# Retention followed by soft mixture-of-experts attention: scaling and transposing the probabilities one step later, with gates, decay, values and the tail rearranged

## The chip, the cores and the metric

One core of one Trainium2 chip. The time is the device time of one execution in microseconds (us), the median of three runs. The core has engines that run their own instruction queues in order: PE (TensorE, matrix products; PEld is its weight load), DVE (VectorE), ACT (ScalarE), POOL (GpSimd) and SP (SyncE, which issues the DMA transfers here). Matrix products land in PSUM, which has eight banks in this kernel; a bank can be used again once its reader has finished.

## The reference

```python
def _attn_ref(q, k, v):                      # 8 batches, 8 heads, 576 tokens, head_dim 64
    scores = scale * np.matmul(q, k.transpose(0, 1, 3, 2))
    gamma = 1.0 - 2.0 ** (-5.0 - np.arange(H))
    Dmat = np.where(rel >= 0, gamma[:, None, None] ** rel, 0.0)
    return np.matmul(scores * Dmat, v)

def _moe_ref(x, w_gate, wq, wk, wv, wo):     # x: (8, 576, 512), 4 experts of width 64
    logits = x @ w_gate                      # the two best experts of each token, softmax over them: w
    for e in range(E):
        q, k, v = x @ wq[e], x @ wk[e], x @ wv[e]
        scores = np.where(causal, -1e9, scale * (q @ k.transpose(0, 2, 1)))
        a = softmax(scores)
        ye = a @ v @ wo[e]
        out += mask[..., None] * w * ye      # where expert e is one of the two
```

All data is 32-bit float. The first half (retention) gives x; the second half (four experts' causal attention with gates) gives the output.

## The kernel before, in words

Each batch of 576 tokens is cut into five chunks (four of 128 tokens, one of 64). The main loop has a step n for each of the 40 chunks, and every instruction of PE, DVE, ACT and POOL runs in the order in which the program writes it; only DMA issues on SP are placed by the compiler.

A step does, in this order. `qk(n)` forms the chunk's retention scores (line 137), ACT copies them out of PSUM as `p` (line 140), POOL masks them (line 143). `result(n-1)` finishes the chunk before: products `old` with the running state and `own` with the chunk's values (lines 165, 178), ACT copies `old` (line 168), DVE adds `own` (line 183), POOL multiplies by the decay table (line 188), ACT rounds to `xh` (line 189) and POOL forms the rest `xl` (line 191). `state(n)` adds the chunk to the running state (PE line 117, DVE lines 123 and 125); it needs `decay(n)`, a POOL multiplication of the chunk's v (line 104) that was written a step earlier, behind line 191. Six steps behind (`LAG = 6`) `scores(n-6)` forms the expert scores `ss` of an attention tile m (line 334, the 64-row tile line 341); DVE masks them and takes maxima (lines 352, 356), ACT takes exponentials with sums (line 360). Then `gates()` runs the whole gate chain on DVE with one ACT exponential in its middle (lines 289 to 308). Then `spread(m)`: three small DVE operations form the factors `rs` (lines 372 to 374), the four expert parts of `p32` are scaled, half on ACT (line 378) and half on DVE (line 380), and DVE transposes them in 32-blocks into the constant tiles TA and TB (lines 385, 387). The scaling is written ahead of the step's remaining PE work, the transposes between its parts.

That PE work (`work(n)`) repeats with five steps for each batch. Five letters name the steps in the text: step K1 (n mod 5 = 1) has the projections kq1 of tokens 256 to 575 (line 233), and the attention values of the batch before (`values`, line 398, evacuated by ACT line 406 and DVE line 407); step V1 (n mod 5 = 2) has the value projections v1 (line 258, evacuated by ACT line 262 and, for the gate logits `lg`, by DVE line 263) and the output projection o0 (line 418, evacuated by ACT line 421); step K0 (n mod 5 = 3) has kq0; step O (n mod 5 = 4) has the output projection o1; step V0 (n mod 5 = 0) has v0. The attention tile of steps K1, V1, K0, O, V0 has t = 0, 1, 2, 3, 4, and its score rows have 64 to 576 elements. In a step with `values` the transposes wait until the values are done, since both use TA. After step 41 a hand-written `end()` takes the last batch's tiles in the order 3, 4, 2.

Of the kernel before, what the change touches and what calls it, by code (L numbers as in the profile page):

```python
# [33 lines left out]
def kernel(ctx: ExitStack, tc: tile.TileContext, xf, xt, vkf, vkt,  # L34
# [111 lines left out]
    def result(n):  # L146
# [39 lines left out]
        yield  # L186
        e = gp if n > 1 else v
        e.tensor_mul(x32, x32, gi[:, :, t0:t0 + C])  # L188
        act(xh[:, :, l0:l0 + C], x32, AF.Copy)  # L189
        yield  # L190
        e.tensor_sub(xl[:, :, l0:l0 + C], x32, f(xh[:, :, l0:l0 + C]))  # L191
# [51 lines left out]
    def vproj(b, r, t):  # L243
# [18 lines left out]
        act(vn[:, ti], ps[:, :E * D], AF.Copy)  # L262
        v.tensor_copy(lg[:, ti], ps[:, E * D:])
        if t == tiles[-1]:
            GATES.append((b, r))

            hv = hbm.tile([128 * nt, E * D], F32, name=f"hv{r}")
            nc.sync.dma_start(hv.rearrange("(t p) c -> p t c", p=128), vn)
            for g in range(4):
                p = g // 2  # L270
                nc.sync.dma_start(vq[QUAD[g]], hv[:, 128 * p:128 * p + 128].rearrange("(j r) c -> r j c", r=32))
# [3 lines left out]
    GATES = []  # L275

    def gates():
        while GATES:
            gate(*GATES.pop())

    def gate(b, r):
        nt = len(RNG[r][2])
# [14 lines left out]
        ex = sb.tile(sh2, F32, name="ex", tag="ex")  # L297
        v.tensor_sub(ex, lg, mx[:, 0].unsqueeze(2).to_broadcast(sh2))
        act(ex, ex, AF.Exp)
        v.scalar_tensor_tensor(ex, rk, 1.5, ex, op0=OP.is_lt, op1=OP.mult)  # L300
        v.tensor_reduce(mx[:, 1], ex, axis=AX.X, op=OP.add)
        v.tensor_scalar(mx[:, 1], mx[:, 1], 1e-9, None, op0=OP.add)
# [62 lines left out]
    def spread(m):  # L365
        b, t = divmod(m, 5)
        r = 0 if t < 2 else 1
        ti = t - RNG[r][2][0]
        p32, sm, ws = SS.pop(m)
        n = len(ws)  # L370
        rs = sm[:, 1, :n]
        v.tensor_scalar(sm[:, 0, :n], sm[:, 0, :n], 1e-9, None, op0=OP.add)
        v.reciprocal(rs, sm[:, 0, :n])
        v.tensor_mul(rs, rs, WT[b, r][:, ti].rearrange("p i z -> p (i z)")[:, :n])  # L374
        for u in range(n):
            x = p32[:, u, :ws[u]]
            if u % 2:
                act(x, x, AF.Copy, scale=rs[:, u:u + 1])  # L378
            else:
                v.tensor_scalar(x, x, rs[:, u:u + 1], None, op0=OP.mult)  # L380
        yield
        for u in range(n):
            z, k, nb = u % 2, 2 * t + u // 2, ws[u] // 32
            x = p32[:, u, :ws[u]].rearrange("p (j c) -> p j c", c=32)
            v.transpose(TA[:, :min(nb, 8), z, k], x[:, :min(nb, 8)])  # L385
            if nb > 8:
                v.transpose(TB[:, :nb - 8, z, k - 4], x[:, 8:])
            yield
# [37 lines left out]

    STEPS = {}
    for b in range(B):
        late = b == B - 1

        for n, kind in ((5 * b + 3, "kq0"), (5 * b + 5 - late, "v0"), (5 * b + 6, "kq1"), (5 * b + 7, "v1"),
                        (5 * b + 11, "y"), (5 * b + 12, "o0"), (5 * b + 14, "o1")):
            if b or kind[-1] == "1" or kind in ("o0", "y"):
                STEPS.setdefault(n, []).append((b, kind, None))
    for n in STEPS:
        STEPS[n].sort(key=lambda x: "kvyo".index(x[1][0]))

# [3 lines left out]
    def work(n):  # L441
        vals = [values(b, 0, 9) for b, kind, part in STEPS.get(n, []) if kind == "y"]
        for b, kind, part in STEPS.get(n, []):
# [3 lines left out]
            if kind[:-1] == "kq":  # L447
                for p in range(2) if part is None else [part]:
                    for w in "kq":
                        yield from proj(b, r, w, p)  # L450
                        for y in vals:
                            next(y, None)
            elif kind[:-1] == "v":
                for t in RNG[r][2] if part is None else [part]:
                    yield from vproj(b, r, t)
            else:
                for d in range(4):
                    yield from outproj(b, r, d)

    def run(g):  # L460
        for _ in g:
            pass


    LAST = NC - 5
    TILES = {n: [n - LAG] for n in range(LAG, NC + 1)}
    TILES[NC].append(LAST)
    TILES[NC + 1] = [LAST + 1]

    def end():  # L470
        b = B - 1
        run(scores(LAST + 3))
        for t in RNG[1][2]:
            run(vproj(b, 1, t))
        for d in range(4):
            run(outproj(b - 1, 0, d))
        gates()
        run(spread(LAST + 3))
        run(scores(LAST + 4))
        for d in range(4):  # L480
            run(outproj(b - 1, 1, d))
        run(spread(LAST + 4))
        run(scores(LAST + 2))
        run(values(b, 0, 4))
        for d in range(4):
            run(outproj(b, 0, d))
        run(spread(LAST + 2))
        run(values(b, 4, 9))
        for d in range(4):
            run(outproj(b, 1, d))  # L490

    warm(12)
    load(0)
# [5 lines left out]
    for n in range(NC + 2):  # L499
# [3 lines left out]
            nc.sync.dma_start(mask[:, 448:], con_d[:, 92:])  # L503
        if n in (1, 4):
            fetch("v" if n == 1 else "o")
        new = TILES.get(n, [])
        late = result(n - 1) if 1 <= n <= NC else iter(())
        if n < 3:

# [7 lines left out]
        else:  # L517
# [2 lines left out]
            next(late, None)  # L520
            if n < NC:
                state(n)
        for m in new[:1]:
            run(scores(m))
        if n > 5:
            run(late)
        decay(n + 1)
        gates()
        for w in {2: "kq", 3: "v", 6: "o"}.get(n, ""):
            weights(w, "l" if w == "k" else "hl")  # L530
        for m in new[1:]:
            run(scores(m))
        new = {NC: new[:1], NC + 1: [LAST] + new}.get(n, new)
        spreads = (None for m in new for _ in spread(m))
        next(spreads, None)
        hold = any(kind == "y" for _, kind, _ in STEPS.get(n, []))
        for _ in work(n):
            if not hold:
                next(spreads, None)
        run(spreads)  # L540
        run(late)
    end()


def _layout(inputs):
# [51 lines left out]
```

## Time and profile before

| | us |
|---|---|
| median of 3 runs | 508.36 |
| lowest and highest | 505.86, 508.96 |
| the profiled execution | 509.4 |
| its span in the trace | 507.7 |

The span runs from the first to the last instruction; 1.7 us of the profiled execution lie around it. In the rows below, PEclk is the granted clock of TensorE as a share of 2.4 GHz; it takes only the two levels 1.0 (2.4 GHz) and 0.5 (1.2 GHz), and a number between them is a mean over a stretch. Square brackets in a timeline give an engine's idle time ahead of the instruction and what ended it.

### The profile page before, as it was taken

How to read it: one execution, taken by the hardware profiler on the slowest of the kernel's cores; microseconds unless marked ns; L12 is line 12 of the kernel's file. 1: busy time of each engine (PE TensorE's matmuls, PEld its weight loads, DVE VectorE, ACT ScalarE, POOL GpSimd, SP SyncE). 2: the span in 40 equal slices, each digit the busy share in tenths (PEclk: the TensorE clock that was granted, in tenths of full speed). 3: DMA queues.
4: the chain of work that ended last, by engine and by line, in shares of the span. 5: the costliest groups of instructions: out<-in, count | busy, mean ns of one | idle time of the engine just before them, and what ended most of it. 6: DMA issues, size and time to landing. Idle time of an engine off the chain costs nothing. (4 is left out here: it accounts for less than half of the span.)

```text
span 507.7 us, 21336 instructions
## 1 busy us (share of the span) xinstructions
PE 434.3 (86%) x9068; PEld 375.5 (74%) x9068; DVE 343.8 (68%) x1275; ACT 258.7 (51%) x802; POOL 174.8 (34%) x198
## 2 busy tenths in 40 slices
PE   6498885799897998699898998699997998889866
PEld 3497873689676997589767897589866886778655
DVE  3744798746888377857788477866788478846750
ACT  2455546526464476536565366536475355645442
POOL 2437354414345233433354143433344153200000
PEclk9579997799998999989988999989988998979879
DMA  8937275214744155433735065432845031300621
GB/s 290 357 104 255 86 178 168 74 35 159 203 151 117 50 160 181 155 89 113 225 113 180 13 200 178 136 107 85 221 138 175 15 105 34 116 3 3 159 70 54
DMA packets 49246, 66.73 MB, mean 131 GB/s; under 512 B 4096, under 2 KB 38400, under 8 KB 49152
## 3 DMA queue, kind: packets, MB, share of 16 engines
q1 hardware_dynamic: 49152, 65.38, 41.1%
q8 instruction: 71, 1.16, 1.0%
q14 instruction: 23, 0.19, 0.1%
HBM read 50.68 MB, written 14.68 MB: 129 GB/s over the span
## 5 line engine op out<-in xcount | busy, mean ns | idle before, releaser
L360 ACT ACTIVATE p<-p,nm 128x64 f32<-128x64 f32 (+6 forms) x144 | 79.5, 553 | 96.6 <-DVE nm L352 65.1
L143 POOL TENSOR_SCALAR_AFFINE_SELECT p<-p 64x512 f32<-64x512 f32 (+1 forms) x80 | 50.1, 626 | 152.2 <-ACT p L140 149.5
L378 ACT ACTIVATE p<-p,sm 128x320 f32<-128x320 f32 (+8 forms) x72 | 36.9, 555 | 62.7 <-DVE sm L374 62.7
L380 DVE TENSOR_SCALAR p<-p,sm 128x320 f32<-128x320 f32 (+8 forms) x72 | 54.2, 789 | 1.4
L352 DVE CUSTOM_DVE_ANT_0 p<-ss,mask 128x128 f32<-128x128 f32 (+7 forms) x128 | 51.0, 452 | 2.8 <-PE ss L334 2.6
L385 DVE STREAM_TRANSPOSE ta<-p 128x256 f32<-128x256 f32 (+2 forms) x144 | 49.8, 368 | 4.4 <-ACT p L378 4.1
L188 POOL TENSOR_TENSOR x<-x,gi 128x512 f32<-128x512 f32 (+1 forms) x38 | 44.3, 1166 | 22.4 <-DVE x L183 17.6
L183 DVE TENSOR_TENSOR x<-x,own 128x256 f32<-128x256 f32 (+1 forms) x80 | 26.1, 358 | 38.1 <-ACT x L168 37.9
L178 PE MATMUL own<-p,vk 64*64 64x64 f32 x1152 | 32.5, 232 | 21.5 <-ACT k L238 14.0
L334 PE MATMUL ss<-k,q 64*64 64x512 f32 (+7 forms) x512 | 48.2, 470 | 2.3 <-DVE nm L356 1.6
L191 POOL TENSOR_TENSOR x1l<-x,x1h 128x512 fp32r<-128x512 f32 (+1 forms) x24 | 26.4, 1099 | 65.6 <-ACT x1h L189 65.6
L407 DVE TENSOR_TENSOR yl<-ys,yh 128x288 fp32r<-128x288 f32 (+2 forms) x36 | 12.8, 416 | 52.1 <-ACT yh L406 52.1
L117 PE MATMUL st<-vk 64*64 64x64 f32 x1024 | 26.1, 232 | 24.4 <-POOL vk L104 14.7
L178 PEld LDWEIGHTS own<-p,vk 64*64 64x64 f32 x1152 | 27.4, 143 | 24.2 <-issue 19.0
L117 PEld LDWEIGHTS st<-vk 64*64 64x64 f32 x1024 | 22.1, 143 | 26.3 <-POOL vk L104 15.4
L398 PE MATMUL ys<-ta,vq 32*64 32x256 f32 (+8 forms) x1152 | 34.7, 369 | 3.8 <-DVE ta L385 2.0
L398 PEld LDWEIGHTS ys<-ta,vq 32*64 32x64 f32 x1152 | 25.6, 141 | 12.2 <-issue 6.9
L104 POOL TENSOR_TENSOR vk<-vk,con 128x512 f32<-128x512 f32 (+1 forms) x34 | 33.4, 984 | 0.1
L418 PE MATMUL po<-yh,who 128*128 128x320 f32 (+1 forms) x128 | 29.6, 312 | 3.3 <-ACT yh L406 3.3
L421 ACT ACTIVATE ot<-po 128x256 f32<-128x256 f32 (+1 forms) x64 | 24.0, 407 | 15.4 <-PE po L418 12.3
L334 PEld LDWEIGHTS ss<-k,q 64*64 64x64 f32 x512 | 23.1, 151 | 9.3 <-DVE nm L356 2.9
L140 ACT ACTIVATE p<-qk 128x256 f32<-128x256 f32 (+1 forms) x80 | 24.7, 368 | 9.9 <-PE qk L137 9.9
(106 smaller groups left out, 1040.1 us busy)
## 6 DMA issues: line engine op xcount, KB each, us to landing
x<-xf SPq DMA_DIRECT2D x32, 512.0 KB, 4.3
vk<-vkf SPq DMA_DIRECT2D x32, 512.0 KB, 5.4
vq<-hv SPq DMA_DIRECT2D x32, 192.0 KB, 4.7
out<-ot SPq DMA_DIRECT2D x32, 160.0 KB, 1.9
vq<-hv SPq DMA_DIRECT2D x32, 128.0 KB, 3.5
out<-ot SPq DMA_DIRECT2D x32, 128.0 KB, 2.5
hv<-vn SPq DMA_DIRECT2D x8, 384.0 KB, 2.9
ta<-wraw SPq DMA_DIRECT2D x4, 512.0 KB, 8.9
```

Of the source, the lines that this page charges most:

```text
L104: (gp if n > 5 else v).tensor_mul(vv, vv, gam[:, 2 * c:2 * c + k].unsqueeze(3).to_broadcast([128, k, 4, D]))
L117: mm(ps[r][HALF[g], s, u], vk[HALF[r], s, 1, h], vk[HALF[r], s, 0, h], start=True, stop=True)
L143: gp.affine_select(w, w, pattern=[[0, 4 * k], [1, 64]], base=0, channel_multiplier=-1, compare_op=OP.is_ge, fill=0.0)
L178: mm(own[r][HALF[u], g, i], vk[HALF[r], s, 0, 2 * g + u], p[HALF[r], g, s, u], start=True, stop=True)
L188: e.tensor_mul(x32, x32, gi[:, :, t0:t0 + C])
L334: mm(ps[u][HALF[p]], q[p][HALF[z], l0 + 64 * i:l0 + 64 * i + 64], k[p][HALF[z], :ws[u]], start=True, stop=True)
L352: v.tensor_tensor_reduce(x, ps[u], mask[:, 512 - ws[u]:], -1.0, BIG, OP.add, OP.min, nm[:, u:u + 1])
L360: act(x, x, AF.Exp, bias=bias, scale=-1.0, accum_out=sm[:, 0, u:u + 1])
L378: act(x, x, AF.Copy, scale=rs[:, u:u + 1])
L380: v.tensor_scalar(x, x, rs[:, u:u + 1], None, op0=OP.mult)
L385: v.transpose(TA[:, :min(nb, 8), z, k], x[:, :min(nb, 8)])
L398: mm(py[g][HALF[z], sj - s0:], vq[QUAD[g], jj, D * z:D * z + D], tt[QUAD[g]], start=(j == 0), stop=(j == 2 * s1 - 1))
```

## The change

- `spread(m)` is issued in the step after that of `scores(m)`, so behind the next tile's maxima and exponentials. Its scaling moves wholly to ACT, save for the two first parts of tiles with t = 3, which stay on DVE. Scaling and transposes are no longer two passes: each part is scaled and transposed, and the parts go between the parts of `work(n)`.
- `gate` becomes a generator that stops behind its ACT exponential; the rest runs a step later.
- `decay(n+1)` is written between POOL's lines 188 and 191, ahead of `xl`.
- `values` of a batch move from step K1 to step V1 of the next batch, beside the value projections; o0 moves from step V1 to step O, and o1 is split between steps O and V0. In the last batch v0 is no longer a step early.
- `end()` and its tile table are replaced by `tail(m)`, which goes through the last tiles in order.

```diff
@@ result
         e.tensor_mul(x32, x32, gi[:, :, t0:t0 + C])
+        if n > 4:
+            decay(n + 2)
         act(xh[:, :, l0:l0 + C], x32, AF.Copy)
@@ gates
-        while GATES:
-            gate(*GATES.pop())
+        for g in GATES[:]:
+            if next(g, True):
+                GATES.remove(g)
@@ gate
         act(ex, ex, AF.Exp)
+        yield False
         v.scalar_tensor_tensor(ex, rk, 1.5, ex, op0=OP.is_lt, op1=OP.mult)
@@ spread
         for u in range(n):
+            z, k, nb = u % 2, 2 * t + u // 2, ws[u] // 32
             x = p32[:, u, :ws[u]]
-            if u % 2:
+            if t == 3 and u < 2:
+                v.tensor_scalar(x, x, rs[:, u:u + 1], None, op0=OP.mult)
+            else:
                 act(x, x, AF.Copy, scale=rs[:, u:u + 1])
-            else:
-                v.tensor_scalar(x, x, rs[:, u:u + 1], None, op0=OP.mult)
-        yield
-        for u in range(n):
-            z, k, nb = u % 2, 2 * t + u // 2, ws[u] // 32
-            x = p32[:, u, :ws[u]].rearrange("p (j c) -> p j c", c=32)
+            x = x.rearrange("p (j c) -> p j c", c=32)
             v.transpose(TA[:, :min(nb, 8), z, k], x[:, :min(nb, 8)])
@@ STEPS
-        for n, kind in ((5 * b + 3, "kq0"), (5 * b + 5 - late, "v0"), (5 * b + 6, "kq1"), (5 * b + 7, "v1"),
-                        (5 * b + 11, "y"), (5 * b + 12, "o0"), (5 * b + 14, "o1")):
+        for n, kind, part in ((5 * b + 3, "kq0", None), (5 * b + 5, "v0", None), (5 * b + 6, "kq1", None),
+                              (5 * b + 7, "v1", None), (5 * b + 12, "y", None), (5 * b + 14, "o0", range(4)),
+                              (5 * b + 14, "o1", range(2)), (5 * b + 15, "o1", range(2, 4))):
@@ work
                     for w in "kq":
                         yield from proj(b, r, w, p)
-                        for y in vals:
-                            next(y, None)
             elif kind[:-1] == "v":
                 for t in RNG[r][2] if part is None else [part]:
                     yield from vproj(b, r, t)
+                    for y in vals:
+                        next(y, None)
@@ end -> tail
-    def end():
+    def tail(m):
         b = B - 1
+        if m < NC:
+            run(scores(m))
         gates()
+        hold = m == NC - 4
+        spreads = spread(m - 1)
+        for n in {NC - 4: (NC + 2,), NC - 3: (NC + 4,), NC - 2: (NC + 5,)}.get(m, ()):
+            for _ in work(n):
+                if not hold:
+                    next(spreads, None)
+        if m == NC - 1:
+            run(values(b, 0, 4))
+            for d in range(4):
+                run(outproj(b, 0, d))
+        run(spreads)
+        if m == NC:
+            run(values(b, 4, 9))
+            for d in range(4):
+                run(outproj(b, 1, d))
@@ main loop
-        for m in new[:1]:
-            run(scores(m))
+        if n >= LAG:
+            run(scores(n - LAG))
         if n > 5:
             run(late)
-        decay(n + 1)
+        else:
+            decay(n + 1)
         gates()
-        spreads = (None for m in new for _ in spread(m))
-        next(spreads, None)
+        spreads = spread(n - LAG - 1) if n > LAG else iter(())
         hold = any(kind == "y" for _, kind, _ in STEPS.get(n, []))
         for _ in work(n):
             if not hold:
                 next(spreads, None)
         run(spreads)
         run(late)
-    end()
+    for m in range(NC - 4, NC + 1):
+        tail(m)
```

## Rows read from the trace of the kernel before

**Rows 1.** Waits of PE over the span (engine, line, waited for: us in total, times, longest).
```profile
PE st L117 <- POOL vk L104: 14.7, 6, 4.8
PE own L178 <- ACT k L238: 14.0, 8, 1.9
```

**Rows 2.** Busy time by window: stretch, length, PE, PEld, DVE, ACT, POOL, PEclk, DMA.
```profile
124.54:414.88 290.34, 260.38 (x5581) 227.29 (x5580) 211.20 (x786) 154.55 (x485) 112.62 (x125) 0.95 0.44 135
...
230.96:241.18 10.22, 10.22 (x205) 9.69 (x204) 7.78 (x31) 6.90 (x22) 4.91 (x5) 1.00 0.40 140
241.18:250.43 9.25, 9.25 (x193) 8.21 (x192) 6.38 (x27) 4.62 (x15) 4.45 (x5) 1.00 0.64 168
250.43:260.91 10.48, 8.65 (x121) 6.63 (x120) 8.17 (x31) 6.99 (x21) 2.80 (x4) 0.84 0.50 185
260.91:268.73 7.82, 6.63 (x138) 5.63 (x137) 7.53 (x24) 3.72 (x12) 3.78 (x5) 1.00 0.59 200
268.73:288.98 20.25, 17.85 (x466) 15.73 (x465) 12.51 (x49) 8.58 (x29) 6.59 (x7) 0.92 0.26 76
```

**Rows 3.** PE's timeline, steps O to K1 of one batch: start, us, instructions, [idle].
```profile
253.19 1.29 PE L178 MATMUL own<-p,vk 64*64 64x64 f32 x30 [1.83 <-ACT k L238]
...
272.54 0.85 PE L117 MATMUL st<-vk 64*64 64x64 f32 x30 [2.40 <-POOL vk L104]
...
273.75 1.44 PE L233 MATMUL pj<-x1h,whk 128*128 128x320 f32 x4
...
277.20 2.85 PE L398 MATMUL ys<-ta,vq 32*64 32x288 f32 x96
...
287.02 0.85 PE L233 MATMUL pj<-x1h,whq 128*128 128x320 f32 x4
```

**Rows 4.** ACT's timeline in steps O and V0 of the same batch.
```profile
251.71 1.07 ACT L378 ACTIVATE p<-p,sm 128x320 f32<-128x320 f32 x2 [3.49 <-DVE sm L374]
...
261.49 1.39 ACT L421 ACTIVATE ot<-po 128x320 f32<-128x320 f32 x4
```

**Rows 5.** DVE's timeline: scaling beside POOL's work, then with POOL idle.
```profile
260.25 2.68 DVE L380 TENSOR_SCALAR p<-p,sm 128x448 f32<-128x448 f32 x2
...
473.20 0.17 DVE L372 TENSOR_SCALAR sm<-sm 128x4 f32<-128x4 f32 x1
...
473.81 0.85 DVE L380 TENSOR_SCALAR p<-p,sm 128x448 f32<-128x448 f32 x2
```

**Rows 6.** The page's groups of instructions: busy us, mean ns of one, idle before.
```profile
L378 ACT ACTIVATE p<-p,sm 128x320 f32<-128x320 f32 (+8 forms) x72 | 36.9, 555 | 62.7 <-DVE sm L374 62.7
L380 DVE TENSOR_SCALAR p<-p,sm 128x320 f32<-128x320 f32 (+8 forms) x72 | 54.2, 789 | 1.4
```

**Rows 7.** ACT and DVE around the last values of a batch, timeline.
```profile
287.52 1.55 DVE L407 TENSOR_TENSOR yl<-ys,yh 128x288 fp32r<-128x288 f32 x4 [5.56 <-ACT yh L406]
...
289.70 0.66 ACT L140 ACTIVATE p<-qk 128x256 f32<-128x256 f32 x2 [0.18 <-PE qk L137]
```

**Rows 8.** Groups of ACT and DVE in the windows of steps O and V0.
```profile
L360 ACT ACTIVATE p<-p,nm 128x448 f32<-128x448 f32 (+1 forms) x4 | 2.7, 686 | 2.0 <-DVE nm L352 2.0
...
L360 ACT ACTIVATION_READ_ACCUMULATOR p<-p,nm 128x1 f32 x4 | 0.8, 188 | 0.0
...
L385 DVE STREAM_TRANSPOSE ta<-p 128x256 f32<-128x256 f32 x8 | 3.3, 410 | 0.0
L352 DVE CUSTOM_DVE_ANT_0 p<-ss,mask 128x448 f32<-128x448 f32 (+1 forms) x4 | 2.5, 655 | 0.5 <-PE ss L334 0.5
...
L387 DVE STREAM_TRANSPOSE tb<-p 128x64 f32<-128x64 f32 (+3 forms) x8 | 2.4, 302 | 0.0
```

**Rows 9.** Busy time by window: steps 6 to 12 (their sum), step 10 and step 11.
```profile
sum 81.75, PE 67.89 PEld 59.70 DVE 59.08 ACT 41.12 POOL 35.50; mean PE 9.70 PEld 8.53 DVE 8.44 ACT 5.87 POOL 5.07
...
79.29:92.13 12.84, 7.79 (x141) 6.08 (x133) 11.05 (x36) 6.60 (x18) 5.88 (x6) 0.73 0.36 121
92.13:114.30 22.17, 18.79 (x465) 16.21 (x464) 12.57 (x49) 8.46 (x29) 6.58 (x7) 0.85 0.22 62
```

More of the change, by code (lines that the diff above doesn't have):

```diff
@@ L264, in vproj @@
         if t == tiles[-1]:
-            GATES.append((b, r))
+            GATES.append(gate(b, r))
             hv = hbm.tile([128 * nt, E * D], F32, name=f"hv{r}")
@@ L428 @@
     for b in range(B):
-        late = b == B - 1
-        for n, kind in ((5 * b + 3, "kq0"), (5 * b + 5 - late, "v0"), (5 * b + 6, "kq1"), (5 * b + 7, "v1"),
-                        (5 * b + 11, "y"), (5 * b + 12, "o0"), (5 * b + 14, "o1")):
+        for n, kind, part in ((5 * b + 3, "kq0", None), (5 * b + 5, "v0", None), (5 * b + 6, "kq1", None),
+                              (5 * b + 7, "v1", None), (5 * b + 12, "y", None), (5 * b + 14, "o0", range(4)),
+                              (5 * b + 14, "o1", range(2)), (5 * b + 15, "o1", range(2, 4))):
             if b or kind[-1] == "1" or kind in ("o0", "y"):
-                STEPS.setdefault(n, []).append((b, kind, None))
+                STEPS.setdefault(n, []).append((b, kind, part))
     for n in STEPS:
@@ L455, in work @@
                     yield from vproj(b, r, t)
+                    for y in vals:
+                        next(y, None)
             else:
-                for d in range(4):
+                for d in part:
                     yield from outproj(b, r, d)
@@ L462, in run @@
             pass
[L465 to L468, printed above, removed]
-    def end():
-        b = B - 1
[L472 to L476, printed above, removed]
-        gates()
[L478 to L490, printed above, removed]
+    def tail(m):
+        b = B - 1
+        if m < NC:
+            run(scores(m))
+        gates()
+        hold = m == NC - 4
[13 more added lines that the diff above has]
+                run(outproj(b, 1, d))
     warm(12)
@@ L505 @@
             fetch("v" if n == 1 else "o")
-        new = TILES.get(n, [])
         late = result(n - 1) if 1 <= n <= NC else iter(())
@@ L530 @@
             weights(w, "l" if w == "k" else "hl")
-        for m in new[1:]:
-            run(scores(m))
-        new = {NC: new[:1], NC + 1: [LAST] + new}.get(n, new)
-        spreads = (None for m in new for _ in spread(m))
-        next(spreads, None)
+        spreads = spread(n - LAG - 1) if n > LAG else iter(())
         hold = any(kind == "y" for _, kind, _ in STEPS.get(n, []))
```

## The prediction

> **What bounds the kernel now.** I read the waits first, then the busy time by window with one window for each step, then the timelines of PE, ACT and DVE where a window is longer than PE's busy time in it. The windows show a kernel of two kinds of stretch [rows 2]. Steps V1 and K0 are PE's alone: its busy time equals their length, 10.22 and 9.25 us. Steps O, V0 and K1 are longer than PE's work: PE idles 1.83, 1.19 and 2.40 us in them, and two of the three windows have a mean clock under 1. The reader is to see that a general share (PE busy 260 of 290 us) hides this: only three of five steps can give anything.
>
> Two waits make up most of that idle time [rows 1]. In step O, `own` waits 1.83 us for a PSUM bank [rows 3]: all eight are held, because the copies of the kq0 projections stand on ACT behind two scalings, and these had waited 3.49 us for the DVE factors [rows 4]. In step K1, `st` waits 2.40 us for POOL's decay [rows 3], which is written behind `xl`.
>
> Each wait is followed by a stretch at 1.2 GHz. Window O's clock of 0.84 means 2 x 0.16 x 10.48 = 3.4 us at the lower level, window K1's 0.92 means 3.2 us [rows 2]. The price can be read: twelve projection matmuls took 277.20 - 273.75 = 3.45 us there and 288.98 - 287.02 = 1.96 us at 2.4 GHz [rows 2, 3], so 1.5 us a time.
>
> So a period of 58.07 us (five in 290.34) [rows 2] holds 5.4 us of idle PE, about 3.3 us of slow clock and some 49.3 us of PE work. That last number stays: the edit removes no matmul. So at most 8.7 us a period can go.
>
> **The change, part by part.** *Scaling to ACT.* 56 of DVE's 72 scalings go. ACT gains 56 x 0.555 = 31 us over the span. DVE loses 54.2 us and keeps 16; two of that width take 0.85 us with POOL idle and 2.68 us beside POOL's work [rows 5, 6], so 7 to 21 us stay and 33 to 47 us go; I take 47, since decay now ends before the scaling starts. The Trainium skill (ScalarE: Activation LUTs, Rules for kernel authors) says the opposite should be done: plain multiplication belongs on VectorE. By that rule the unlocked 0.43 us [rows 5] against ACT's mean of 0.555 us [rows 6] would make the move a loss of about 0.1 us a part; the trace agrees on the lone instruction and not on its place beside POOL. Neither total sets the end; the place in the queues does.
>
> *Scaling a step later.* The sums that the factors need are then a step old, so the 3.49 us of ACT's wait go and with it the 1.83 us in step O. *Gates in halves* takes away DVE's wait for ACT inside the chain; DVE is covered in steps K1, V1 and K0, so by itself I cost it at nothing, and at about 0.5 us a period in step O if that cover fails. *Decay ahead of `xl`* removes the 2.40 us: POOL no longer waits for ACT's `xh` first. `xl` gets one decay later, some 1 us, and the projection that reads it is two steps on.
>
> What is late next? I walked the queues through a period, counting from the end of the last `values` matmul, with at most eight banks in use.
>
> (a) *Start of step K0.* Today the last values are followed by one more projection, which covers their evacuation. Now nothing follows. The four `yl` end 289.07 - 287.02 = 2.05 us later [rows 3, 7]; behind them DVE forms the held-back factors, 473.81 - 473.20 = 0.61 us [rows 5], and ACT scales four small parts (an estimate of 1.4 us, under the mean of 0.555 each), before it may copy the new `p` (0.33 us each) [rows 6, 7]. So the banks for `ss` come at 4.4 to 4.7 us, while PE could use them at 1.9: **2.8 us**. If the banks came from elsewhere it would be the 0.8 us until `yl` frees two for `own`.
>
> (b) *Step O.* `own` finds its banks almost in time, **0.4 us**; 0 to 1.8.
>
> (c) *Step V0.* ACT in step O now has four exponentials with sums (3.5 us) [rows 8], then six output copies (1.39 / 4 = 0.35 each) and four scalings (about 0.54 each) in turn: 4.2 us [rows 4]. The maxima (2.5 us) [rows 8] start about 3.8 us into the step, behind the copies that (a) made late; exponentials end near 8.0, `xh` at 8.6, the chain at 12.8. PE's own work in that step is 8.4 us; its next `st` needs the last two output banks, and `ss` the `p` copies behind them. PE gets to the value projections 14.7 us in instead of 11.8: **2.9 us**. Bounds: 0, if PE finds free banks; 4.2, the whole chain.
>
> (d) *Start of step K1.* `own` needs the banks of the value projections, and DVE's copy of `lg` stands behind the eight transposes of the longest tile, 2.65 us (out of the 5.7 us for two tiles [rows 8]) and two scalings of 0.85 [rows 5]: **1.9 us**; 0 to 3.5.
>
> *Transfers.* The output copies take their transfers along, and the transfer into `vq` (one buffer for tokens 256 to 575) now waits on SP for the last `values`. Chunk loads queue behind it, but for two steps later: I cost this at nothing; if that cover fails, decay is late again, at up to today's 2.40 us. Six output copies in step O share four buffers; (c)'s upper bound holds that.
>
> Together 8.0 us where 5.4 us go. The slow clock: falls behind (a) and (c) would come where ACT and DVE set the pace, so most of their 1.5 us is hidden; I count none, and 1.5 each as the other bound. A period is 49.3 + 8.0 = **57.3 us** against 58.07: 4 us less over five periods.
>
> *Start-up.* Steps 6 to 12 take 81.75 us with 67.89 us of busy PE, the clock at 0.73 and 0.85 in steps 10 and 11 [rows 9]: 13.9 us idle and 2 x (0.27 x 12.84 + 0.15 x 22.17) = 13.6 us slow, worth 6.8. In steps 9 to 11 there is little PE work, and DVE is busy 11.05 of 12.84 us [rows 9]. The same walk leaves one wait of 4 us in step 10 (`ss` behind the scalings), 2 us in step 11 and 1 to 2 us of slow clock. One output projection (3 us) leaves these steps for later. 81.75 - 3 - 13.9 - 6.8 + 7.5 + 2.5 (waits of parts under 0.5 us) = 68: **13.8 us less**; bounds 6 and 19.
>
> *Tail.* From step 38 on the kernel takes 507.7 - 414.88 = 92.8 us [rows 2]. Three microseconds of output projection come in. In the plain order the longest tile is scaled and transposed with nothing beside it, and the last tile behind it; the walk gives 96.3 us: **3.5 us more**; 0 to 8.
>
> Sum: 507.7 - 13.8 - 4 + 3.5 = 493.4 us of span, 495.1 with the 1.7 us around it. The profiled execution (509.4) lies 1.0 us over the median (508.36), so I predict **494 us**.
>
> **The rivals.** *All waits hidden.* If the compiler hands out banks so that (a), (c) and (d) shrink to half, the period is 53 us, 21 us less over five: about 473 us. For it: a bank goes to whoever is next when it is free, and I assumed every one held to the end. Against it: eight banks were already full in step O.
>
> *The gain is used up on ACT.* ACT's chain per period grows by 6 us. If copies and scalings run at their lone lengths (about 0.1 us more each, 14 in a period) and the start gains only its lower bound of 6 us, the period is 58.7 and the sum 507.7 - 6 + 3.2 + 3.5 = 508.4 us of span, about 509: no change that can be told. One measurement of this kernel can tell about 1% from no change.
>
> *The slow clock, on the other side.* PE runs at 1.2 GHz after waits of 1.83 and 2.40 us [rows 3]. If it falls at (a), (c) and (d) of each period and the slow stretches are not hidden, each costs 1.5 us: 4.5 us x 5 periods and twice 4.5 at the ends make 31 us, hence 525 us. It decides from two unhidden falls a period on, since they cost 15 us over five periods and the gain to lose is 14.3. For it: (a) and (c) leave PE short bursts between waits. Against it: kq0 and v0 behind them end before ACT and DVE are ready for the next step. [...]
>
> **How the numbers follow.** My forecast (484 to 503) has 0.55, the first rival 0.14, the second 0.16, the third 0.15. The range 474 to 514 leaves out the fastest part of the first, most of the third: 2 in 10. Faster by over 1% (under 503.3) has 0.55 + 0.14 = 0.69; within 1%, 0.17, with the upper edge of the second and the mildest of the third; slower 0.14.
>
> **What would show it.** In the profile after: no wait of `own` for ACT's k copies, none of `st` for POOL's decay; a wait of `ss` for ACT's `p` of 1.5 us or more at each start of step K0; ACT's output copies and scalings in turn, with `st` or `own` in step V0 waiting for them; DVE's scaling at 16 instructions of under 0.5 us; steps 9 to 11 shorter by 8 us or more; the tail no shorter. The forecast is wrong if the period is under 54 or over 59 us, if steps 9 to 11 don't shrink, or if the clock falls more than twice a period in stretches where PE is busy throughout.

## The result, and the profile after

The changed kernel takes 481.05 us (median of 4 runs, 479.09 to 482.98); the kernel before took 508.55 us beside it (4 runs, 505.86 to 508.96). The ratio is 0.947, with a 95% interval of 0.9417 to 0.9522: 5.3% faster. The prediction was 494 us in a range of 474 to 514. The time lies in the range and on the forecast side, but 13 us under the forecast and under the likeliest case's own 484 to 503. Of the runs of all variants below one (478.78 us, of the last variant) fell in a slow state of the chip, at a granted clock of 0.83, and is left out of that variant's time.

The profiled execution of the changed kernel took 481.82 us, its span 478.3 us. Lines have moved: the scaling is now line 385 on ACT and 383 on DVE, the factors 376 to 378, the transposes 387 and 389, the gate's exponential 302, `xl` 193, the copies of k and q 240 and 242.

Busy time by window of the changed kernel (columns as in [rows 2]): steps 6 to 12, the five periods, everything from step 38 on, then one period step by step: O, V0, K1, V1, K0.

```profile
42.42:112.86 70.44, 61.85 (x1426) 54.90 (x1425) 47.94 (x197) 40.34 (x129) 35.19 (x40) 0.95 0.44 135
112.86:383.08 270.22, 253.87 (x5587) 222.89 (x5581) 184.79 (x750) 166.12 (x520) 112.10 (x125) 0.98 0.47 145
383.08:478.30 95.22, 79.57 (x1377) 65.89 (x1372) 54.88 (x227) 52.90 (x157) 9.31 (x11) 0.89 0.25 73
...
178.73:186.51 7.78, 7.78 (x134) 6.41 (x133) 6.24 (x23) 5.46 (x18) 4.15 (x5) 1.00 0.38 137
186.51:196.84 10.33, 8.79 (x149) 7.53 (x148) 7.83 (x30) 7.40 (x21) 4.04 (x6) 1.00 0.60 186
196.84:206.87 10.03, 9.96 (x178) 9.44 (x177) 8.97 (x38) 6.58 (x23) 4.90 (x5) 1.00 0.58 165
206.87:220.56 13.69, 13.69 (x470) 11.96 (x469) 5.21 (x26) 5.46 (x19) 4.87 (x5) 1.00 0.24 82
220.56:232.18 11.62, 10.31 (x202) 9.02 (x197) 8.71 (x37) 8.23 (x27) 4.47 (x5) 1.00 0.66 195
```

The three stretches are those of [rows 9] and [rows 2]. Start-up: 81.75 became 70.44 us, 11.3 less. Five periods: 290.34 became 270.22, 20.1 less. From step 38 on: 92.8 became 95.2, 2.4 more. Together 507.7 - 11.3 - 20.1 + 2.4 = 478.7, against 478.3 measured; the remaining 0.4 us lie ahead of step 6.

In the five periods PE's idle time fell from 290.34 - 260.38 = 29.96 to 270.22 - 253.87 = 16.35 us, so 13.6 us of the gain is idle time. The other 6.5 us is PE's own busy time: the same matmuls ran less often at 1.2 GHz (mean clock 0.95 before, 0.98 after). The batch shown above has the clock at 1.00 throughout. In step V0 of three of the five batches it falls (means of 0.85, 0.85 and 0.86), and the step takes 11.5 to 11.9 us there instead of 10.33.

The scaling, in the groups of instructions of the changed kernel:

```profile
L385 ACT ACTIVATE p<-p,sm 128x128 f32<-128x128 f32 (+7 forms) x128 | 63.4, 539 | 23.1 <-DVE sm L378 23.1
...
L383 DVE TENSOR_SCALAR p<-p,sm 128x448 f32<-128x448 f32 x16 | 8.5, 531 | 0.3
```

ACT carries 128 scalings instead of 72 and yet waits less for the factors, 23.1 us instead of 62.7 [rows 6]. DVE keeps 16.

The waits of PE in the changed kernel:

```profile
PE own L178 <- issue: 5.6, 7, 2.7
PE ss L338 <- ACT p L140: 4.5, 4, 1.3
PE ss L345 <- ACT p L140: 4.5, 1, 4.5
...
PE own L178 <- ACT ot L423: 3.2, 6, 0.7
PE st L117 <- issue: 3.1, 7, 1.3
```

Both large waits of [rows 1], 14.7 and 14.0 us, are gone from the top of the list. Smaller ones stand in their place, and PE's timeline shows where: at the start of step K0, in step V0 (four times), and in step K1.

```profile
224.62 1.68 PE L338 MATMUL ss<-k,q 64*64 64x320 f32 x16 [1.28 <-ACT p L140]
...
241.09 0.45 PE L165 MATMUL old<-x,s 64*64 64x64 f32 x12 [0.39 <-ACT ot L423]
241.86 0.33 PE L178 MATMUL own<-p,vk 64*64 64x64 f32 x4 [0.32 <-issue]
242.68 0.45 PE L178 MATMUL own<-p,vk 64*64 64x64 f32 x12 [0.49 <-ACT ot L423]
243.47 0.90 PE L117 MATMUL st<-vk 64*64 64x64 f32 x30 [0.34 <-issue]
...
252.62 0.62 PE L178 MATMUL own<-p,vk 64*64 64x64 f32 x26 [1.04 <-DVE lg L265]
```

### The profile page after: what moved, and what is told of

It reads as the page before. It is cut to its first block, busy times and chain, and to the rows that moved or that the text cites. A ratio compares the mean times of both kernels' runs of the same rounds, so it can differ in the third digit from the quotient of the medians.

```text
span 478.3 us, 21378 instructions
## 1 busy us (share of the span) xinstructions
PE 425.9 (89%) x9068; PEld 369.6 (77%) x9068; DVE 307.7 (64%) x1219; ACT 278.4 (58%) x858; POOL 172.4 (36%) x198
## 5 line engine op out<-in xcount | busy, mean ns | idle before, releaser
L364 ACT ACTIVATE p<-p,nm 128x64 f32<-128x64 f32 (+5 forms) x144 | 79.5, 553 | 76.9 <-DVE nm L356 56.2
L143 POOL TENSOR_SCALAR_AFFINE_SELECT p<-p 64x512 f32<-64x512 f32 (+1 forms) x80 | 48.8, 610 | 166.8 <-ACT p L140 164.2
L385 ACT ACTIVATE p<-p,sm 128x128 f32<-128x128 f32 (+7 forms) x128 | 63.4, 539 | 23.1 <-DVE sm L378 23.1
L387 DVE STREAM_TRANSPOSE ta<-p 128x256 f32<-128x256 f32 (+2 forms) x144 | 56.0, 394 | 28.9 <-ACT p L385 26.2
L338 PE MATMUL ss<-k,q 64*64 64x64 f32 (+7 forms) x512 | 41.0, 408 | 4.5 <-ACT p L140 4.5
L400 PE MATMUL ys<-ta,vq 32*64 32x288 f32 (+7 forms) x1152 | 35.4, 375 | 6.5 <-DVE ta L387 4.4
L178 PEld LDWEIGHTS own<-p,vk 64*64 64x64 f32 x1152 | 26.3, 137 | 15.7 <-issue 14.9
L264 ACT ACTIVATE vn<-pv 128x256 f32<-128x256 f32 x40 | 14.8, 371 | 39.5 <-PE pv L260 39.5
L265 DVE COPY lg<-pv 128x4 f32<-128x4 f32 x40 | 5.9, 149 | 43.9 <-ACT vn L264 43.4
L117 PEld LDWEIGHTS st<-vk 64*64 64x64 f32 x1024 | 23.1, 145 | 10.8 <-issue 4.2
L420 PEld LDWEIGHTS po<-yh,who 128*128 128x128 f32 x128 | 20.9, 194 | 10.4 <-issue 4.9
```

Of the source, the lines that this page charges most:

```text
L117: mm(ps[r][HALF[g], s, u], vk[HALF[r], s, 1, h], vk[HALF[r], s, 0, h], start=True, stop=True)
L143: gp.affine_select(w, w, pattern=[[0, 4 * k], [1, 64]], base=0, channel_multiplier=-1, compare_op=OP.is_ge, fill=0.0)
L178: mm(own[r][HALF[u], g, i], vk[HALF[r], s, 0, 2 * g + u], p[HALF[r], g, s, u], start=True, stop=True)
L338: mm(ps[u][HALF[p]], q[p][HALF[z], l0 + 64 * i:l0 + 64 * i + 64], k[p][HALF[z], :ws[u]], start=True, stop=True)
L364: act(x, x, AF.Exp, bias=bias, scale=-1.0, accum_out=sm[:, 0, u:u + 1])
L400: mm(py[g][HALF[z], sj - s0:], vq[QUAD[g], jj, D * z:D * z + D], tt[QUAD[g]], start=(j == 0), stop=(j == 2 * s1 - 1))
```

## The experiments

Twelve variants were run. Each ratio is against runs of the kernel before on the same chip, with its 95% interval. Three parts of the change were never tried alone or undone alone: the scaling a step later, the move of `values`, and the tail in plain order.

### Which part carries the gain

**The gate chain whole again.** In the changed kernel:

```diff
-        for g in GATES[:]:
-            if next(g, True):
-                GATES.remove(g)
+        while GATES:
+            for _ in GATES.pop():
+                pass
```

> The changed kernel with the gate chain whole again, in the step after its projection. Theory of the queues: the factors of step K0 stand behind a gate chain that waits for an exponential at the end of ACT's queue, so scaling and the projection copies come 2 us later, own in step O waits again for some 1 us; 484 to 489 us. Rival, that a chain with slack around it costs nothing: 480 to 483 us.

Measured: 502.0 us, ratio 0.9897 (0.9866 to 0.9928). This one edit gives back 21 of the 27.5 us. PE's waits and the timeline of steps K0 and O show the old stall, in the new order:

```profile
PE own L178 <- ACT k L240: 13.8, 8, 2.0
```

```profile
237.95 0.61 ACT L191 ACTIVATE x1h<-x 128x512 fp32r<-128x512 f32 x1
238.47 0.20 ACT L302 ACTIVATE ex<-ex 128x12 f32<-128x12 f32 x1
238.64 1.28 POOL L193 TENSOR_TENSOR x1l<-x,x1h 128x512 fp32r<-128x512 f32 x1 [2.26 <-ACT x1h L191]
238.70 1.25 DVE L304 SCALAR_TENSOR_TENSOR ex<-rk,ex 128x12 f32<-128x12 f32 x1 [0.74 <-ACT ex L302]
...
241.30 0.17 DVE L376 TENSOR_SCALAR sm<-sm 128x4 f32<-128x4 f32 x1
...
241.92 0.80 ACT L385 ACTIVATE p<-p,sm 128x192 f32<-128x192 f32 x2 [3.25 <-DVE sm L378]
...
243.13 0.33 PE L178 MATMUL own<-p,vk 64*64 64x64 f32 x4 [1.96 <-ACT k L240]
```

Read the second list from the top. The gate's small exponential comes to ACT behind the tile's four exponentials and `x1h`, so DVE waits 0.74 us for it. Line 304 then takes 1.25 us: POOL is running `x1l` meanwhile, and both end at 239.9. The rest of the chain follows, and the factors begin at 241.30. ACT has waited 3.25 us for them, against 3.49 us in the kernel before [rows 4], and `own` waits 1.96 us, against 1.83 [rows 3]. Yet the sums that these factors use are a full step old here. So the stall in step O did not come from the age of the sums, but from the gate chain that stood ahead of the factors on DVE.

The halves can't be tried alone in the kernel before: the gates of v1 are formed in step K0, and there the factors of the tile with t = 2, which need them, are formed in the same step. The scaling a step later is what makes the halves possible.

**The gate chain behind the step's work, in the kernel before.** `gates()` moves from ahead of `spread` to the end of each step:

```diff
         decay(n + 1)
-        gates()
@@
         run(spreads)
         run(late)
+        gates()
```

> The kernel before with one edit: the whole gate chain is called at the end of the step that makes the logits, and no longer between the maxima and the factors of the next step; everything else, the scaling in its own step too, stays. Theory of the gate chain: the factors of step K0 are ready about 3 us sooner, so ACT's scaling no longer waits 3.49 us and own in step O no longer 1.83 us; with the clock 3 us a period, 490 to 498 us. Rival, my prediction's reading: the factors wait for the sums of the same step's exponentials, so own still waits over 1 us, 503 to 509 us.

Measured: 514.05 us, ratio 1.0152 (1.0116 to 1.0189): 1.5% slower. **The same with decay ahead of `xl`:**

> The kernel before with decay ahead of the rest (alone 490.4 us) and the gate chain written at the end of its own step (alone 514.1 us, slower, though it emptied the bank wait of step O). Theory, that the gate chain at the end lost its gain because POOL's decay was the next thing late (st waited 3.35 to 3.63 us in K1 there): with decay ahead the bank wait of O is gone and no wait of 3 us stands in K1, so the two add up to 474 to 484 us. Rival, that the gate chain at the end itself delays DVE's and ACT's work at the start of the next step (own's 1.59 us in V0): the gain of O goes there again, and the time stays at 490 to 500 us.

Measured: 496.2 us, ratio 0.9791 (0.9764 to 0.9818), 6 us slower than decay ahead alone (below). Windows of steps O and K1, first of the variant without decay ahead, then with it:

```profile
253.25:259.94 6.69, 6.69 (x121) 5.33 (x120) 5.71 (x20) 4.48 (x16) 2.69 (x4) 1.00 0.65 236
269.43:292.04 22.61, 18.79 (x466) 16.48 (x465) 13.62 (x49) 8.54 (x29) 6.61 (x7) 0.85 0.22 64
```

```profile
244.33:251.03 6.70, 6.70 (x122) 5.33 (x121) 5.54 (x22) 4.86 (x17) 3.12 (x4) 1.00 0.54 194
259.09:281.67 22.58, 19.23 (x466) 16.52 (x465) 12.03 (x49) 8.81 (x29) 5.59 (x6) 0.85 0.29 93
```

Step O falls from 10.48 [rows 2] to 6.69 and 6.70 us: without the gate chain ahead of the factors the stall is gone, which confirms the reading above from the other side. But K1 grows from 20.25 [rows 2] to 22.6 us in both. The timeline of the second variant shows a part of why:

```profile
263.16 0.19 DVE L265 COPY lg<-pv 128x4 f32<-128x4 f32 x2
...
264.46 0.21 ACT L301 ACTIVATE ex<-ex 128x8 f32<-128x8 f32 x1 [1.96 <-DVE ex L300]
264.57 0.64 ACT L140 ACTIVATE p<-qk 128x256 f32<-128x256 f32 x2
```

The gate's exponential now stands on ACT ahead of the new chunk's `p` copies and waits 1.96 us for DVE, whose chain stands behind the transposes of the longest tile. Of the 2.3 us that the step grows, 1.0 is idle time of PE: `ss` waits 0.47 us for those `p` copies, and `st` waits 2.88 us instead of 2.40, until DVE's `lg` copies (above) are done. The other 1.4 us is PE's busy time, 19.23 us instead of 17.85, at a mean clock of 0.85 instead of 0.92. The chain was moved whole, and its one ACT instruction went on blocking ACT, in another step. Cut in two, as in the change, the first half reaches ACT behind the exponentials and the second half, a step later, needs nothing from it.

**Decay ahead of `xl` alone, in the kernel before.**

```diff
         e.tensor_mul(x32, x32, gi[:, :, t0:t0 + C])
+        if n > 4:
+            decay(n + 2)
@@
         if n > 5:
             run(late)
-        decay(n + 1)
+        else:
+            decay(n + 1)
```

> The kernel before with one part alone: decay ahead of xl. Undoing it in the changed kernel cost nothing. Theory of the gate chain (formed on that run): st waited for POOL because xh came late behind ACT's other work; putting decay ahead takes the 2.40 us wait of step K1 away here, but PE runs into the next bank wait in that step; 500 to 506 us. Rival, my prediction's costing: 2.4 us and a fall of the clock a period go, 484 to 492 us. Rival: no change, 507 us or more.

Measured: 490.4 us, ratio 0.9683 (0.9655 to 0.9711): 16.5 us. **And undone in the changed kernel:**

```diff
-        if n > 4:
-            decay(n + 2)
@@
         if n > 5:
             run(late)
-        else:
-            decay(n + 1)
+        decay(n + 1)
```

> The changed kernel (481.05 us) with one part undone: decay stands behind xl again. Theory of the queues (mine): in step K1 st waits for POOL again, at 2.4 us a period or somewhat less since xh is now ready earlier; with a fall of the clock every other time that is 2 to 3 us a period, 488 to 496 us. Rival, that this one line carries most of the gain: 498 us or more, and the fall of the clock in each K1. Rival, that the scaling's move alone freed POOL: under 484 us.

Measured: 480.1 us, ratio 0.9474 (0.9437 to 0.951): within a microsecond of the changed kernel's 481.05. The same edit is worth 16.5 us before the others and nothing behind them. How it gains alone is not what the prediction said; PE's waits, DVE's scalings, and the windows of the five periods and of two K1 steps, in the kernel before with decay ahead:

```profile
PE st L117 <- issue: 14.9, 6, 2.9
...
L382 DVE TENSOR_SCALAR p<-p,sm 128x320 f32<-128x320 f32 (+8 forms) x72 | 39.4, 584 | 1.4
```

```profile
119.49:397.42 277.93, 251.91 (x5581) 219.88 (x5581) 199.91 (x785) 155.14 (x485) 112.02 (x125) 0.98 0.45 141
201.02:219.72 18.70, 16.42 (x465) 14.41 (x465) 12.03 (x49) 8.69 (x29) 5.61 (x6) 1.00 0.34 98
255.90:276.44 20.54, 17.63 (x465) 15.21 (x465) 12.07 (x50) 8.82 (x29) 5.60 (x6) 0.92 0.33 103
```

`st` still waits 14.9 us in six places, as in [rows 1]; only the name POOL is gone from them. In the first of the two K1 steps shown it waits 2.28 us, in the second 2.91. Idle time falls by only 4 us over the five periods (277.93 - 251.91 = 26.0, from 29.96), while PE's busy time falls by 8.5 us, from 260.38 to 251.91, and the mean clock rises from 0.95 to 0.98. So two thirds of the 12.4 us that the periods lose is the clock. The trace names nothing that `st` waits for there, but the times tell. First the kernel before, in the K1 step of [rows 3], then the second K1 step with decay ahead:

```profile
270.69 1.04 POOL L104 TENSOR_TENSOR vk<-vk,con 128x512 f32<-128x512 f32 x1
...
272.05 0.66 ACT L140 ACTIVATE p<-qk 128x256 f32<-128x256 f32 x2
```

```profile
260.00 0.19 DVE L265 COPY lg<-pv 128x4 f32<-128x4 f32 x2
...
260.23 0.70 PE L117 MATMUL st<-vk 64*64 64x64 f32 x32 [2.91 <-issue]
```

In the kernel before, decay ended at 271.73, and `st` began at 272.54 [rows 3], 0.8 us later and 0.49 us behind the start of ACT's `p` copies. With decay ahead `st` begins 0.04 us behind the end of the `lg` copies in the step shown, and 0.48 us behind the start of the `p` copies in the shorter of the two waits (204.80 against 204.32). So in that step of the kernel before decay wasn't what `st` waited for to the end, although the trace put it down to POOL. These copies free banks and stand behind the longest tile's scaling and transposes, so the wait is for a bank; this follows from the order in time, no releaser shows it. It also fits that the edit is worth nothing in the changed kernel, where that tile is scaled a step later.

What the edit did take away is DVE's meeting with decay: the mean of DVE's 72 scalings falls from 789 [rows 6] to 584 ns. Whether this is what kept the clock up wasn't tried.

### What the move of the scaling to ACT costs

**Even parts on DVE again, in the changed kernel**, still a step late:

```diff
-            if t == 3 and u < 2:
+            if u % 2 == 0:
                 v.tensor_scalar(x, x, rs[:, u:u + 1], None, op0=OP.mult)
```

> The changed kernel with the even parts scaled on DVE again, a step late and part by part. Theory of the queues: ACT's chain in step O gets shorter by two scalings (1.1 us) but each DVE scaling that meets POOL's xl takes 1.3 us more and the transposes and lg copies stand behind it; the two about cancel, 480 to 487 us, and DVE's scalings have a mean over 0.6 us. Rival, that ACT's load sets the pace: 474 us or less. Rival, that freeing DVE was the gain: 490 us or more.

Measured: 465.1 us, ratio 0.9168 (0.9131 to 0.9204): 16 us faster than the changed kernel. The two scaling groups, the windows of the five periods and of one step V0 in this variant:

```profile
L385 ACT ACTIVATE p<-p,sm 128x64 f32<-128x64 f32 (+8 forms) x72 | 39.0, 555 | 24.0 <-DVE sm L378 24.0
...
L383 DVE TENSOR_SCALAR p<-p,sm 128x64 f32<-128x64 f32 (+8 forms) x72 | 30.2, 419 | 1.4
```

```profile
110.13:371.41 261.28, 250.47 (x5587) 219.83 (x5581) 194.22 (x785) 153.45 (x485) 112.35 (x125) 0.99 0.49 150
...
234.95:243.86 8.91, 8.47 (x150) 7.36 (x149) 8.00 (x33) 6.19 (x18) 3.83 (x6) 1.00 0.68 210
```

The same 72 DVE scalings that took 789 ns each [rows 6] now take 419 ns. Decay ahead alone brought them to 584 ns (above); the rest came with the other edits, most likely with the scaling's place a step later, where it seldom falls together with POOL's work; no run has that place alone. The move to ACT was not needed for it. With the move, ACT copies six output tiles and scales four parts in turn, V0 takes 10.33 us instead of 8.91 even where the clock holds (in three of the five batches it falls, above), and PE idles 16.35 us over the five periods instead of 261.28 - 250.47 = 10.8. The periods account for 9 of the 16 us (270.22 against 261.28); the rest lies ahead of them (112.86 against 110.13) and behind.

**Both edits, even parts on DVE and the gate chain whole:**

> The changed kernel with both of the edits tried alone before: the gate chain whole again (alone +21 us over the changed kernel) and the even parts scaled on DVE again (alone -16 us). Theory, that the whole chain stalls ACT's queue in front of the k copies however the scaling is divided: the 21 us come on top of the split version's 465, so 484 to 488 us, with own waiting for ACT's k copies again some 8 times, over 10 us in total. Rival, that the whole chain hurts only because ACT carries nearly all scalings and has no slack: with half of them gone the chain costs a third or less, 466 to 473 us, and own's wait stays under 5 us.

Measured: 481.8 us, ratio 0.9496 (0.9465 to 0.9527). The whole chain costs 16.7 us here and 21 us where ACT has the scalings. So neither expectation is met exactly; most of the stall is the chain's own, and about a fifth of it hangs on ACT's load. `own` waits for ACT's k copies in 6 places, 9.2 us in all.

**The held-back scalings ahead of the work in step V1, in the changed kernel.** Where the transposes wait for the values, the four scalings don't have to.

```diff
@@ spread
...
+        if ahead:
+            for u in range(n):
+                scale(u)
+            yield
...
```

> The changed kernel with one more edit: in the step that holds its transposes back for the values, the four scalings are written ahead of the step's work, only the transposes wait. Theory of the queues: ss in step K0 waits 1.3 us for ACT's p behind these scalings, and with own and st step K0 is 2.4 us longer than PE's work; 1.2 to 2.4 us a period and in the tail go, 468 to 474 us. Rival, that the banks held by the yl evacuation set that wait: 478 to 482 us.

Measured: 476.5 us, ratio 0.9396 (0.935 to 0.9441): 4.5 us less, though the two intervals overlap a little. **Together with the even parts on DVE:**

> The changed kernel with the even parts scaled on DVE again (as in the run of 465.1 us) and the held-back scalings written ahead of the step's work (as in the run of 476.5 us). If the two waits are apart, ss in step K0 and the banks of step V0, the gains add up: 459 to 462 us. Rival, that both shorten the same queue of ACT: 464 to 466 us.

Measured: 461.2 us, ratio 0.9096 (0.9064 to 0.9127), 4 us less than with the even parts alone. **And with `xh` and `xl` behind the step's work as well** (the generator of `result` stops once more, behind decay, and goes on at the step's end):

```diff
             decay(n + 2)
+            yield
@@
         if n > 5:
-            run(late)
+            next(late, None)
```

> The run before with one more edit: xh and xl of a chunk are written behind the step's work. Theory of the queues: DVE's last factor operation no longer meets POOL's xl (0.375 us a time instead of 0.16) and ACT's copies come 0.6 us sooner, 456 to 460 us, and the mean of that operation falls under 0.2 us. Rival: xl is needed by the next step's projections and they wait for it, 463 us or more.

Measured: 460.65 us, ratio 0.9092 (0.9057 to 0.9126): no different from the one before, although DVE's factor operation (line 378, there 379) no longer meets POOL's `xl` and falls from a mean of 373 to 162 ns. These two are the fastest versions of the study, 9% under the kernel before and 4% under the changed one. The window of step K0 with the scalings ahead, all else as changed:

```profile
218.91:228.71 9.80, 9.77 (x197) 8.74 (x192) 8.24 (x35) 7.57 (x25) 4.45 (x5) 1.00 0.74 222
```

It is 9.80 us instead of 11.62. So the wait at K0's start is that of the `p` copies behind the held-back scalings. The gain isn't the same in each batch: of the five K0 steps four took 9.8 to 11.1 us and one 13.32, where `own` waited 2.12 us and the clock fell (a mean of 0.87).

### Where the output projections stand

**o0 back in step V1, o1 whole in step O, in the changed kernel:**

```diff
-(5 * b + 14, "o0", range(4)), (5 * b + 14, "o1", range(2)), (5 * b + 15, "o1", range(2, 4))
+(5 * b + 12, "o0", range(4)), (5 * b + 14, "o1", range(4))
```

> The changed kernel with the output projections where the kernel before had them: o0 in step V1 behind the values, o1 whole in step O. Theory, that placing o0 and o1 beside the longest tiles is what keeps PE supplied in steps O and V0: PE gets 1.5 to 3 us less work there and waits for DVE and ACT instead, steps O and V0 together lose less than the 3 us that step V1 gains, and o0's first product waits 1 to 2 us for the copies of the values: 485 to 495 us. Rival, that the placement is indifferent because o0 covers the 1.3 us that ss waits at the start of step K0 and ACT's six output copies no longer hold banks in V0: 474 to 484 us.

Measured: 492.4 us, ratio 0.9714 (0.9684 to 0.9745): 11 us slower than the changed kernel. Windows of steps V1, K0 and V0, and one of PE's waits:

```profile
209.72:228.18 18.46, 17.32 (x494) 14.98 (x493) 7.45 (x34) 8.09 (x27) 4.88 (x5) 1.00 0.34 106
228.18:237.77 9.59, 9.59 (x193) 8.52 (x192) 6.90 (x31) 7.35 (x25) 4.46 (x5) 1.00 0.73 203
...
244.47:254.29 9.82, 7.93 (x137) 6.58 (x136) 7.81 (x28) 6.11 (x18) 4.18 (x6) 0.83 0.58 175
```

```profile
PE po L420 <- ACT yh L408: 13.9, 16, 6.6
```

Step K0 loses its wait (9.59 us), but o0's products now wait for the copies of the values, and V0 has 7.93 us of PE work in 9.82 us with the clock at 0.83. Placing output projections beside the longest tiles is part of the gain.

**o1 whole in step V0, with the even parts on DVE and the scalings ahead:**

```diff
-(5 * b + 14, "o1", range(2)), (5 * b + 15, "o1", range(2, 4))
+(5 * b + 15, "o1", range(4))
```

> The version with even parts scaled on DVE and the held-back scalings ahead (461.2 us), with o1 whole in step V0 instead of half in O, half in V0. Theory, that what is left of the waits in V0 comes from six output copies between ACT's scalings in O: with four there, old and own wait under 0.5 us in V0 and PE has more to do beside the longest tile: 455 to 460 us. Rival, that PE runs short in step O instead, whose own work is then one output projection, and the copies stand in the way of st and own in K1: 463 to 470 us.

Measured: 463.8 us (median of three runs), ratio 0.9149 (0.9125 to 0.9173), about 2.5 us slower than the split in halves; the two intervals just touch. The wait that it was to remove was hardly there any more: in the base version `own` waits for output copies 0.2 us in all, since ACT scales only half of the parts there. What came is a new one, five waits of `st` in step V0 of up to 1.2 us, 6.0 us in all. The trace puts them down to POOL's `x1l`; but in the one looked at, `x1l` ended at 234.11 and `st` began at 235.10, while ACT was copying output tiles. Step O is short there (6.27 us), so V0 reaches `st` early. That the output copies hold its bank is argued from these times, not shown.

## Why the prediction was right, and where it was not

**Which steps can give anything.** This held for two of the three. PE's idle time in step O, 1.83 us, is gone, and that in K1, 2.40 us, is down to 0.07 us in the batch shown. V0 gave nothing: PE idles 1.54 us there, 1.19 before. K0, full before, now idles 1.31 us. The rest of the gain lies in the start-up and the clock.

**Size of the period.** Predicted 57.3 us, measured 270.22 / 5 = 54.04: over five periods 20.1 us less, not 4. This is the mis-sized term; start-up (11.3 less, predicted 13.8) and tail (2.4 more, predicted 3.5) came within 2.5 us. The period was built as 49.3 us of PE work plus 8.0 us of new waits. (The 5.4 us of old waits taken off it are one batch's; the five hold 29.96 / 5 = 6.0.) Measured, it is 253.87 / 5 = 50.8 of PE busy and 16.35 / 5 = 3.3 of waits. The waits were found in their places and called too long (measured: the step's length against PE's work in it, or against the step before):

| place | predicted | measured |
|---|---|---|
| (a) start of K0 | 2.8 | 2.4 (11.62 against 9.25 us), 1.28 of it idle, `ss` waiting for the `p` copies |
| (b) `own` in step O | 0.4 | 0 (window O has no idle PE) |
| (c) V0 behind ACT's copies and scalings | 2.9 | 1.5 (four waits of 0.3 to 0.5), and 1.2 to 1.6 more where the clock falls, in three of five batches |
| (d) K1, `own` behind `lg` | 1.9 | about 0 in four of five batches (10.03 us, 9.96 busy, in the one shown), 1.04 in the next |

(c) and (d) are the two that fail, and with them the assumption that each of the eight banks stays held to the end of its chain. In (c) PE waited four times, twice for an output copy by the trace and twice for nothing that it names, and each wait was short: ACT's chain ran on beside PE's work, where the prediction let the whole chain stand once. In direction the first rival (waits at half, a period of 53 us) was nearer than the forecast: 54.04 us is just above it.

**The signs it named.** `own` no longer waits for ACT's k copies, ACT's output copies and scalings stand in turn ahead of V0's waits, and the tail is no shorter. Steps 9 to 12 together take 8.9 us less (12.3 less in steps 9 to 11, whose values moved to step 12). Two signs missed: `ss` waited 1.28 us at most in K0, where 1.5 or more was named, and DVE's 16 scalings took 0.53 us, not under 0.5. By its own words the forecast is wrong under a period of 54 us; it measured 54.04. So the time in the range is in part luck: two parts were priced wrongly with opposite signs, the halves of the gate chain at nothing (21 us) and the scaling on ACT without a price of its own (16 us the other way).

**Gates in halves.** "By itself I cost it at nothing" is the step that failed outright, and no number in the sum showed it, since the 1.83 us in step O was credited to the scaling a step later. With the chain whole 21 us come back. The evidence was in the kernel before: ACT's 3.49 us wait for the factors [rows 4] ended in a DVE operation, and the prediction followed it to the sums' age without walking DVE's queue back through the gate chain, written ahead of the factors.

**Scaling to ACT.** "Neither total sets the end; the place in the queues does" is right, and it speaks against this part: what stands in ACT's queue is what the move costs, 16 us. The rule that the prediction weighed and set aside, in the Trainium skill (ScalarE: Activation LUTs, Rules for kernel authors), that plain multiplication belongs on VectorE, agrees with these runs: 465.1 us with half of the parts on DVE, 481.05 with nearly all on ACT. That DVE's scalings would lose their long duration beside POOL's work without the move was not seen.

**Decay ahead.** That the edit "removes the 2.40 us" is the second step that failed: in the step of [rows 3] decay had ended 0.8 us before `st` began, and with decay ahead `st` waits as long without it. The edit gains two thirds of what the periods lose by the clock, in the kernel before alone; in the changed kernel it is worth nothing. The wait is gone from the changed kernel all the same, most likely because the longest tile is scaled a step later, behind the `p` copies; no run has that alone.

**The slow clock.** The third rival, that it falls at (a), (c) and (d) of each period, came in part: it fell at (c) in three of five batches and not at (a) or (d). The mean clock in the five periods still rose from 0.95 to 0.98, since the falls in O and K1 went. Twice 0.02 of 270.22 us, about 11 us, were run at the lower level, against twice 0.05 of 290.34, about 29 us, before. The prediction let most of a fall at (c) be hidden; in V0 it cost 1.2 to 1.6 us each time.

## What to carry to other kernels

When an engine waits for a small result, walk the producing engine's queue back past everything written ahead of it: a short chain that crosses to another engine and back stalls both in-order queues, and cutting it at the crossing was worth 21 us here, where moving it whole made the kernel before 1.5% slower. Where work is long only because it falls together with another engine's, take the overlap away before moving the work: with decay earlier and the scaling later DVE's scalings took 419 ns instead of 789, and the move to ACT cost 16 us. Before curing a wait, check that the named instruction ends where the wait ends: decay had ended 0.8 us earlier. Two edits that each look like the cure of one wait can be worth 16 us or nothing, depending on which comes first, so undo each part of a bundle and also do it alone.

## What the hardware showed that was not expected

**A tiny DVE operation can cost over a microsecond.** In the changed kernel the factor operation was moved to where POOL forms the rest:

```profile
238.87 1.28 POOL L193 TENSOR_TENSOR x1l<-x,x1h 128x512 fp32r<-128x512 f32 x1 [1.60 <-ACT x1h L191]
239.07 1.10 DVE L378 TENSOR_TENSOR sm<-sm,wt 128x4 f32<-128x4 f32 x1
...
240.21 0.56 ACT L385 ACTIVATE p<-p,sm 128x320 f32<-128x320 f32 x1 [1.15 <-DVE sm L378]
```

Four elements to a partition took 1.10 us and ended as POOL's operation did (240.17 and 240.15); ACT waited 1.15 us for it. In step K0 of the same batch, at 222.93 and 230.16 us, the same operation took 0.16 us. The Trainium skill (SBUF — State Buffer, Who interferes with whom) says that a DVE instruction with two inputs in SBUF contends with a GpSimd instruction that reads SBUF; these rows agree. In them, and in line 304 above (12 elements, 1.25 us), the small operation lasted until POOL's ended. It need not cost time: without the meeting the variant with `xh` and `xl` late was no faster.

**The same wait did and did not bring the clock down.** In the kernel before with decay ahead, K1 steps took 18.70 us at a clock of 1.00 behind a wait of `st` of 2.28 us and 20.54 us at 0.92 behind one of 2.91, and the kernel before fell behind 2.40 us [rows 3]. In step O of the kernel before, the batch ahead of the one in [rows 3] shows the opposite; PE's timeline, and the window of that step:

```profile
195.86 0.89 PE L178 MATMUL own<-p,vk 64*64 64x64 f32 x30 [1.87 <-ACT k L238]
```

```profile
193.06:202.07 9.01, 7.14 (x122) 5.72 (x121) 7.20 (x29) 6.27 (x19) 2.12 (x3) 1.00 0.46 163
```

Behind a wait of 1.87 us the clock stayed at 1.00 and the step took 9.01 us; a batch later it fell behind 1.83 us, and the step took 10.48 [rows 2, 3]. A fall is worth 1.5 us of a step here, and the length of the wait ahead of it doesn't tell whether it comes: a model that prices a wait by its length alone misses most of what decay ahead gained in the five periods.
